# A queue of double score steps across pairs of head pairs, with other filler, score-buffer and rank settings, in attention followed by a low-rank mixer

## The chip, the cores and the metric

The kernel runs on one NeuronCore of a Trainium2 chip; the other cores are unused. The metric is the device time of one execution in microseconds (us), as a median of several. The profile's span, from the first to the last instruction, is a little shorter than that time: the profiled execution took 614.26 us and its span is 612.5 us.

Engine names are those of the profile: PE is TensorE (matmuls; PEld is its weight load), DVE is VectorE, ACT is ScalarE, POOL is GpSimd, SP is SyncE, which here only issues transfers.

## The reference

Attention with a threshold, for 8 batches, 8 heads, 576 rows and head width 64, and behind it a mixer on the 512 joined columns:

```python
scores = scale * q @ k.T                      # 576 x 576 for each of 64 heads
thresh = max(scores) - tau                    # per row
scores = where(scores >= thresh, scores, -1e9) - max(scores)
attn = exp(scores);  attn /= sum(attn) + 1e-09
x = attn @ v                                  # heads joined: 8 x 576 x 512
h = (x.T @ U @ V).T                           # low rank, 32, over the rows
u = x + h
out = u + relu(u @ w_ch1) @ w_ch2             # 512 -> 2048 -> 512
```

Inputs and output are float32. Row maxima have to be exact enough to decide what passes the threshold, so q times k is done in float32; the rest of the matmuls are bf16, v as two bf16 parts.

## The kernel before

The unit of the attention part is a **head pair** (two heads of one batch): four per batch, 32 in all, `p` from 0 to 31. A head pair has 576 rows: four tiles of 128 rows and one of 64; the two 64-row tiles of a pair of head pairs (`p`, `p + 1`) share a step. So each pair of head pairs has nine **score steps**, and the kernel has 144.

The kernel is not written in the order in which it runs. Python code makes a list of tasks, each with an engine, a modelled cost and what it depends on; a list scheduler then picks, engine by engine, what comes next, and only then are the instructions recorded, in that order. What is recorded is fixed: at run time each engine goes through its own list in order and waits on semaphores.

```python
class Order:
    TO_PE = 0.15
    BEGIN = (1.2, 4.5, 0.7, 1.3, 0.7)         # PE, DVE, ACT, POOL, SP: free from
    HOLD = (84.27, 20.8, 39.99, ...)          # one number for each of 9 phases
    KEPT = ((), (0, 1, 3, 4), (0, 1, 2, 3, 4, 5))   # PSUM banks of a step: none, one, two
    OFF = { "copy_main": (19.13, -43.29, ...), ... }   # a rank for each kind of task and phase
    ...
        def rank(c):
            ...
            return (t.ready + t.off, s)       # the smallest goes first
    ...
            if e == PE:
                n = free[0]
                while at[PE] + 0.45 < s and last[n] <= at[PE]:
                    self.filler(n)            # a matmul whose result nobody reads
                    at[PE] += 0.22 if at[PE] > 5.5 else 0.43
```

The filler is `fill`, one bf16 matmul of 128x512 with the identity, recorded wherever the model expects PE to idle for over 0.45 us. It keeps PE's clock up and computes nothing.

A score step writes two scores tiles (one for each head) to PSUM. A **double** step does two of them in one go, over all six PSUM banks of the two `trio` tiles; a **single** step uses four banks. Each step has 16 matmuls of 64x64 on the array's quadrants:

```python
    def score_tasks(*steps):                  # one or two steps (p, i)
        def scores(_):
            for slot, (p, i) in enumerate(steps):
                for piece in range(2):
                    for j in range(2):
                        for h in range(2):
                            ...
                            nc.tensor.matmul(cols[part, lo:hi], a.tT[hs, 0, rows],
                                             a.tT[hs, 1, lo:hi], start=True, stop=True)   # L584
        S_ = add(PE, 0.96 * len(steps), scores, deps, kind="S", ...)
        for slot, (p, i) in enumerate(steps):
            step_tasks(p, i, slot, S_, len(steps))
```

Behind it come, for each of the step's two tiles, three passes over 128x576:

```python
    NS = 6
    s_ring = ring("s_sb", NS, [P, S], FP32)
    e_ring = ring("e_sb", NS, [P, S])                    # bf16
    ...
            def weigh(_, ...):                           # DVE, L613: PSUM -> s_sb, and the row's extreme
                nc.vector.tensor_scalar(out=s_sb, in0=score_cols(slot, x), ..., accum_out=m[:, x:x + 1])
            t = add(VEC, 0.678, weigh, [S_, got("w", tiles[0] + x - NS)], frees=[...])
        ...
            def exponential(_, ..., e_sb=e_ring[tiles[0] % NS], s_sb=s_ring[tiles[0] % NS]):   # ACT, L636
                nc.scalar.activation(out=e_sb, in_=s_sb, func=ACT.Exp, ...)
            ex = add(SCA, 0.667, exponential, [mins[x], got("w", tiles[0] - NS)])
            def select(_, ...):                          # DVE, L643: threshold, product, row sum
                nc.vector.scalar_tensor_tensor(out=w_sb[:, 0:S], in0=s_sb, scalar=thr_[:, x:x + 1],
                    in1=e_sb, op0=ALU.is_le, op1=ALU.mult, accum_out=pr.den[:, i, x:x + 1])
```

`got("w", n)` is the `select` of tile `n`: a tile may take a score buffer only once the `select` that read it last is done.

The selected tiles are transposed by DMA (early on some by PE), then multiplied with v (`product`, L743 to L751, in `value_tasks`), normalized, pushed through the low-rank part, and fed to the mixer's two big products, `up` (L916; `rest`, L932, is its 64-row remainder) and `down` (L949), in `mixer_tasks`. They have 1,088 matmuls of 128x512 and can fill PE wherever a batch is ready for them; `DUE`, one number for each batch, says from which PE step on.

The order in which the tasks are made:

```python
    LONE = 2
    for p in range(0, NP, 2):
        prepare_tasks(p)                      # load q, k, v; transpose q and k on PE
        prepare_tasks(p + 1)
        nine = [(p, i) for i in range(NT)] + [(p + 1, i) for i in range(4)]
        n = 0
        while n < 9:
            two = p >= LONE and n             # the first of nine stays single
            score_tasks(*nine[n:n + (2 if two else 1)])
            n += 2 if two else 1
        value_tasks(p)
        value_tasks(p + 1)
        if (p + 1) % NPAIR == NPAIR - 1:
            mixer_tasks(p // NPAIR)
```

Nine is odd, so each pair of head pairs has one single step and four double ones (the first pair has nine single ones).

Of the kernel before, what the change touches and what calls it, by code (L numbers as in the profile page):

```python
# [68 lines left out]
P = 128  # L69
# [6 lines left out]
B, H, S, D = 8, 8, 576, 64  # L76
# [5 lines left out]
NT = 5  # L82
# [8 lines left out]
W1_AT = (1, 4, 6, 9, 11, 14, 16, 19)  # L91
W2_AT = (20, 21, 23, 24, 25, 26, 28, 29)

DUE = (7.75, 80, 1258.25, 220, 779.25, 421.75, 107.5, 873)

# [30 lines left out]
class Order:  # L128
# [3 lines left out]
    LAG = (0.0, 0.07, 0.1, 0.06, 0.0)  # L132
    SLOW = (1.0,) * 5
    TO_PE = 0.15
    BEFORE = 0.45
    PATIENCE = (0, 0.2, 0.1, 0.9, 1.35)


    BEGIN = (1.2, 4.5, 0.7, 1.3, 0.7)
    LANES = 8  # L140
    SHARE = (0.6, 0.4)
    LANDING = (3.1, 1.4)
    SWITCH = {"quadrants": 0.17, None: 0.13}
    PARTS = {"S": "quadrants"}

    HOLD = (84.27, 20.8, 39.99, 23.29, 62.35, 18.34, 53.51, 0.13, 43.1)
    KEPT = ((), (0, 1, 3, 4), (0, 1, 2, 3, 4, 5))


    OFF = {  # L150
        "copy_main": (19.13, -43.29, -8.12, 1.42, -28.78, -25.28, -22.95, 51.41, -45.85),
        "copy_rest": (60.73, 4.11, 41.5, -5.4, -29.64, 13.18, -80.58, -82.36, -26.38),
        "copy_tt": (198.41, -75.7, -33.86, 48.32, 43.85, 100.62, 7.39, -22.81, -38.44),
        "copy_u": (-21.98, 23.28, 116.5, 77.07, -33.95, 19.36, 29.03, -92.86, 6.98),
        "copy_u4": (-14.02, 51.4, 17, 17.47, -40.5, -60.28, -41.34, 103.29, 7),
        "copy_w": (-55.25, -15.23, 222.13, -81.81, -37.73, 188.9, 52.5, -41.28, 57.53),
        "down": (-108.85, 30.21, -20.13, 90.15, -87.01, -79.16, -34.24, -44.29, 29.17),
        "exponential": (-31.87, -48.96, 9.03, -42.56, 174.18, 12.19, 450.6, 189.09, 141.41),
        "finish": (28.37, -76.92, -41.93, 101.63, 56.59, 2.69, -121.7, -34.02, -50.98),
        "first": (-17.99, 10.62, -38.53, 2.6, 67.74, -65.5, 2.83, -19.66, -6.62),  # L160
        "high": (66.93, -13.94, 46.69, 712.1, 60.2, 95.3, 89.97, 88.03, 39.14),
        "inverse": (-26.26, 8.92, 39.77, 95.96, 39.08, 91.45, 463.65, 19.36, 0.65),
        "join": (13.52, 6.42, 53.64, 9.45, 3.36, 1.67, -114.73, 2.82, 39.08),
        "load": (-18.74, 67.06, -50.44, 55.17, 58.64, 82.33, 125.87, 149.78, -25.84),
        "low": (-9.73, -27.81, 40.61, -12.77, 5.4, -48.88, -55.07, -5.58, -26.87),
        "low4": (41.75, 36.85, 84.8, 33.79, 11.84, -6.69, 54.93, 183.24, 6.02),
        "low_part": (34.11, -32.17, 4.8, -1.24, -37.88, -65.32, -18.36, -17.94, 32.22),
        "low_rank": (-14.94, 306.57, -9.99, 33.17, -60.48, -12.24, -11.83, -46.7, -6.24),
        "make": (7.68, -10.52, -21.46, 3.08, -3.94, 16.95, -45.27, 13.88, 128.85),
        "narrow": (-0.28, -20.88, -40.1, -70.82, 16.79, -28.72, 19.58, 6.78, 1.71),  # L170
        "narrow_u": (-40.8, 31.47, -51.68, -32.58, -91.27, -26.3, 41.16, 82.58, 150.13),
        "narrow_u4": (14.28, 67.11, -13.63, 38.96, 69.08, -15.88, 47.54, -1.08, 25.04),
        "norm": (-36.47, 20.94, 161.35, 153.52, 17.7, 32.05, 16.49, -33.48, 39.64),
        "product": (-25.78, 3.36, 107.07, 34.07, -42.31, 23.71, 434.46, 110.74, -31.94),
        "relu": (44.83, -56.9, 29.43, 68.16, -76.53, 48.16, -10.98, -65.64, 20.44),
        "rest": (8.59, -53.71, 2.63, -9.48, -11.11, -0.73, -28.87, -55.87, 44.85),
        "scores": (-93.28, 8.57, -18.04, -47.28, 8.63, -52.95, -23.78, 413.25, 12.79),
        "select": (46.36, 293.14, 35.49, 104.01, 268.55, 52.2, 72.98, 458.57, 76.64),
        "send": (-23.34, 51.64, 92.04, 28.49, 36.91, 7.91, -217.4, 116.71, -45.23),
        "spread": (-102.39, 8.5, 9.39, -103.02, -0.46, -2.66, -90.25, 41.8, -45.93),  # L180
        "spread4": (26.63, -29.14, -107.73, -80.42, 55.43, 21.3, 10.43, -96.64, -100.01),
        "spread_v": (-62.05, 41.65, -47.22, -27.41, -38.59, 71.83, -165.61, -55.1, -78.6),
        "sum_u": (-55.36, 122.9, 45.74, 86.89, 15.92, 19.31, 4.11, 28.68, 42.79),
        "sum_u4": (15.44, 21.98, -56.37, 5.74, -50.96, -32.03, -61.24, 1.51, 8.11),
        "sums": (27.18, -39.86, -41.27, 101.93, 22.18, 54.82, -48.56, -32.18, -32.56),
        "threshold": (21.67, 39.75, 57.31, -114.62, 90.56, 114.55, -29.79, 46.4, 15.18),
        "turn4": (-47.62, -15.25, -30.68, 42.71, -53.87, -22.98, 35.92, 44.06, 19.31),
        "turn_main": (34.7, -53.42, 3.16, -104.58, -21.66, 79.99, 120.4, 29.72, 83.93),
        "turn_pe": (64.97, 45.46, -130.42, 85.1, 783.71, 163.63, -9.74, -23.06, 24.73),
        "turn_rest": (-89.01, 57.73, -34.88, -49.83, -30.63, 450.94, -36.86, -120.61, -31.99),  # L190
        "turn_u": (45.94, -3.77, -33.34, -53.57, -41.76, -35.51, 29.3, 1351.91, -155.36),
        "turn_w": (27.84, 6.6, -10.51, -30.89, 13.25, 5.13, -98.42, -39.84, 75.01),
        "twin": (4.39, -28.65, 54.86, 6.83, 27.36, 37.94, -39.09, -43.19, -45.42),
        "up": (49.2, -4.95, -54.97, 27.94, 3.9, 179.31, 88.49, -14.97, -39.78),
        "values": (-4.75, -11.18, -30.87, -20.21, -89.93, -8.58, 33.05, 56.9, 16.01),
        "weigh": (16.47, -218.81, -43.72, 80.8, 58.98, -59.6, -10.99, 13.81, 42.45),
        "weights": (-138.85, 46.32, -104.74, -59.99, 22.37, -4.15, 9.01, -37.1, -40.33),
    }

    def __init__(self, nbanks, filler):  # L200
# [2 lines left out]
    def add(self, *args, **kw):  # L203
        t = Task(*args, **kw)
        t.phase = self.phase
        t.lag = 0.0 if t.dma else self.LAG[t.engine]
        t.off = self.OFF[t.fn.__name__][self.phase]
        self.tasks.append(t)
        return t

    def run(self):
# [25 lines left out]
        while left:  # L237
# [28 lines left out]
            if e == PE:  # L266
                n = free[0]
                while at[PE] + 0.45 < s and last[n] <= at[PE]:
                    self.filler(n)
                    at[PE] += 0.22 if at[PE] > 5.5 else 0.43  # L270
                    last[n] = at[PE]
                    kind = "fill"
                parts = self.PARTS.get(t.kind)
                if parts != self.PARTS.get(kind):
                    s += self.SWITCH[parts]
                kind = t.kind
# [30 lines left out]
            steps += t.steps  # L307
            for a in t.after:
                a.ready = max(a.ready, t.end + (self.SIGNAL[e] + (0.0 if a.engine else self.TO_PE)
                                           if a.engine != e or t.dma else 0.0) -  # L310
                              (a.lead if e == PE or e == VEC and a.steps else 0.0))
                a.left -= 1
                if not a.left:
                    ready[a.engine].append(a)
# [4 lines left out]
def kernel(  # L319
# [61 lines left out]
    def ring(name, n, shape, dtype=BF16):  # L381
        return [wpool.tile(shape, dtype, name=f"{name}{k}") for k in range(n)]
# [1 line left out]
    qkraw_ring = ring("qkraw", 2, [P, 9, 2, D], FP32)  # L384
    qkT_ring = ring("qkT", 2, [P, 2, S], FP32)
    vh_ring = ring("vh", 2, [P, NT, 2, 2, D])
    NS = 6
    s_ring = ring("s_sb", NS, [P, S], FP32)
    e_ring = ring("e_sb", NS, [P, S])
    m_ring = ring("m", 8, [P, 2], FP32)  # L390
    thr_ring = ring("thr", 8, [P, 2], FP32)
    rec_ring = ring("rec", 4, [P, NT, 2], FP32)
# [208 lines left out]
    def step_tasks(p, i, slot, S_, len_):  # L601
# [30 lines left out]
        thr = add(SCA, 0.19, threshold, mins)  # L632

        for x in range(2):
            def exponential(_, x=x, e_sb=e_ring[tiles[0] % NS], s_sb=s_ring[tiles[0] % NS]):
                nc.scalar.activation(out=e_sb, in_=s_sb, func=ACT.Exp, bias=m[:, x:x + 1],  # L636
                                     scale=-1.0)

            ex = add(SCA, 0.667, exponential, [mins[x], got("w", tiles[0] - NS)])

            def select(_, x=x, w_sb=w_ring[n % (NW // 2)][:, x, :], e_sb=e_ring[tiles[0] % NS],
                       s_sb=s_ring[tiles[0] % NS]):
                nc.vector.scalar_tensor_tensor(  # L643
                    out=w_sb[:, 0:S], in0=s_sb, scalar=thr_[:, x:x + 1], in1=e_sb,
                    op0=ALU.is_le, op1=ALU.mult, accum_out=pr.den[:, i, x:x + 1])
# [385 lines left out]
            piece(W2_AT[c], lambda _, c=c: w2(_, c), 0.7, weights2, 2.0)  # L1031

    weight_loads()
    for p in range(0, NP, 2):
        prepare_tasks(p)
        prepare_tasks(p + 1)
        nine = [(p, i) for i in range(NT)] + [(p + 1, i) for i in range(4)]
        n = 0
        while n < 9:
            two = p >= LONE and n  # L1040
            score_tasks(*nine[n:n + (2 if two else 1)])
            n += 2 if two else 1
        value_tasks(p)
        value_tasks(p + 1)
        if (p + 1) % NPAIR == NPAIR - 1:
            mixer_tasks(p // NPAIR)

# [37 lines left out]
```

## Time and profile before

| | |
|---|---|
| time, median of 3 | 615.04 us (613.98 to 615.18) |
| span of the profiled execution | 612.5 us, PE clock full throughout |
| PE busy | 588.1 us (96%), of which fillers (L418) 23.2 us, 82 matmuls |
| DVE busy | 522.0 us (85%) |
| ACT busy | 467.6 us (76%) |
| POOL busy | 364.9 us (60%) |
| score matmuls (L584) | 2,304, first at 10.9 us, last at 543.0 us |
| DVE `select` (L643) and `weigh` (L613) | 288 each, 238.9 and 203.1 us |

PE's row says 96% for a stage in which it does useful work and for one in which it runs fillers, so it is to be read stage by stage, and with the filler's line beside it. Matmul ends in the trace are modelled, and neighbours overlap; the distance from the start of one group of matmuls to the start of the next is the better measure of what a group costs.

### The profile page before, as it was taken

What the parts mean: (1) busy time and instruction counts of PE and PEld (TensorE: products, weight loads), DVE (VectorE), ACT (ScalarE), POOL (GpSimd) and SP (SyncE); (2) the same over time, 40 slices, a digit from 0 to 9 for tenths busy, and PEclk for the clock granted to TensorE, in tenths of its full rate; (3) what the DMA queues carried; (4) which work ended last, traced back from release to release, by engine and by line L of the source; (5) the groups of instructions that cost most, each with busy time, mean ns of one, the idle gap of its engine ahead of it and who ended that gap; (6) DMA issues with size and microseconds to landing.
All of it is one profiled execution on the core that took longest, in us unless ns stands there. A gap on an engine that the chain in (4) does not pass through costs nothing. (4 is left out here: it accounts for less than half of the span.)

```text
span 612.5 us, 17223 instructions
## 1 busy us (share of the span) xinstructions
PE 588.1 (96%) x6267; PEld 354.1 (58%) x6343; DVE 522.0 (85%) x1399; ACT 467.6 (76%) x983; POOL 364.9 (60%) x596
## 2 busy tenths in 40 slices
PE   7989889999999999999999999999999999999996
PEld 3446565666566655565566665556565656456553
DVE  2999997998989999899998997999998999994101
ACT  3858898998699876897789965898698977885540
POOL 7768776777777757576666665576557643323000
PEclk9999999999999999999999999999999999999999
DMA  6799999666799799868998998878887897656203
GB/s 148 119 157 164 171 159 176 128 129 145 162 165 164 135 169 172 173 129 145 178 171 141 159 166 159 164 117 156 185 145 156 140 159 143 125 93 102 46 16 70
DMA packets 209716, 87.35 MB, mean 143 GB/s; under 512 B 187744, under 2 KB 199984, under 8 KB 209632
## 3 DMA queue, kind: packets, MB, share of 16 engines
q1 hardware_dynamic: 194624, 63.15, 62.6%
q0 software_dynamic: 14048, 22.76, 18.8%
q8 instruction: 50, 0.82, 0.6%
q10 hardware_dynamic: 960, 0.34, 0.2%
q14 instruction: 34, 0.28, 0.2%
HBM read 37.90 MB, written 9.44 MB: 77 GB/s over the span
## 5 line engine op out<-in xcount | busy, mean ns | idle before, releaser
L636 ACT ACTIVATE e_sb<-s_sb,m 128x576 bf16<-128x576 f32 x288 | 218.5, 778 | 42.9 <-DVE s_sb L613 42.2
L643 DVE SCALAR_TENSOR_TENSOR w_ring<-s_sb,thr,e_sb 128x576 bf16<-128x576 f32 x288 | 238.9, 858 | 9.2 <-ACT e_sb L636 5.9
L613 DVE TENSOR_SCALAR_CACHE_REDUCE s_sb<-trio 128x576 f32<-128x576 f32 x288 | 203.1, 750 | 22.5 <-PE trio L584 20.2
L584 PE MATMUL trio<-qkT 64*64 64x288 f32 (+2 forms) x2304 | 164.2, 410 | 1.3 <-DVE x L772 0.3
L661 POOL COPY w_ring<-w_ring 128x128 bf16<-128x128 bf16 (+1 forms) x168 | 72.0, 433 | 128.8 <-DVE w_ring L643 101.7
L584 PEld LDWEIGHTS trio<-qkT 64*64 64x64 f32 x2304 | 83.3, 133 | 58.9 <-issue 7.0
L949 PE MATMUL bank<-W2b,R 128*128 128x512 bf16 x400 | 98.8, 379 | 2.1 <-DVE x L830 0.6
L455 POOL DMA_DIRECT2D qkraw<-in_q_dram x125 | 82.3, 662 | 31.0 <-PE bank L515 25.5
L455 POOL DMA_DIRECT2D qkraw<-in_k_dram x125 | 81.2, 654 | 4.7 <-issue 4.1
L949 PEld LDWEIGHTS <-R 128*128 128x128 bf16 x576 | 53.3, 98 | 53.0 <-issue 2.5
L916 PE MATMUL bank<-uT,W1b 128*128 128x512 bf16 x327 | 81.5, 380 | 0.7
L795 POOL TENSOR_TENSOR x<-x,rec 128x256 f32<-128x256 f32 (+1 forms) x84 | 63.1, 752 | 30.0 <-DVE x L788 23.0
L916 PEld LDWEIGHTS <-W1b 128*128 128x128 bf16 x512 | 47.4, 98 | 57.2 <-issue 6.3
L747 PEld LDWEIGHTS <-wT_ring 128*128 128x128 bf16 x896 | 55.5, 98 | 9.3 <-issue 4.9
L550 POOL TENSOR_TENSOR vh<-vraw_ring,vh 64x128 bf16<-64x128 f32 x64 | 55.7, 870 | 5.5 <-ACT vh L543 0.8
L906 ACT ACTIVATE R<-bank 128x512 bf16<-128x512 f32 x90 | 52.3, 601 | 4.6 <-PE bank L916 3.7
L961 DVE TENSOR_TENSOR o<-bank,x 128x512 f32<-128x512 f32 x27 | 18.5, 685 | 34.1 <-remote 20.4
L747 PE MATMUL bank<-vh,wT_ring 128*128 128x128 bf16 x608 | 43.6, 220 | 1.8 <-POOL vh L550 1.2
L629 ACT ACTIVATE thr<-m,tau_t 128x2 f32<-128x2 f32 x144 | 42.5, 297 | 0.9 <-DVE s_sb L613 0.6
L916 PE MATMUL trio<-uT,W1b 128*128 128x512 bf16 x150 | 38.6, 379 | 1.5 <-issue 0.2
L949 PE MATMUL trio<-W2b,R 128*128 128x512 bf16 x136 | 33.4, 379 | 1.1 <-DVE s_sb L613 0.8
L906 ACT ACTIVATE R<-trio 128x512 bf16<-128x512 f32 x54 | 32.3, 600 | 2.2 <-PE trio L916 1.1
(104 smaller groups left out, 749.4 us busy)
## 6 DMA issues: line engine op xcount, KB each, us to landing
out_dram<-o SPq DMA_DIRECT2D x71, 128.0 KB, 2.6
vraw_ring<-in_v_dram SPq DMA_DIRECT2D x32, 160.0 KB, 3.6
qkraw<-in_k_dram POOLq DMA_DIRECT2D x63, 80.0 KB, 4.5
qkraw<-in_q_dram POOLq DMA_DIRECT2D x62, 80.0 KB, 3.9
vraw_ring<-in_v_dram SPq DMA_DIRECT2D x32, 128.0 KB, 4.2
qkraw<-in_q_dram POOLq DMA_DIRECT2D x63, 64.0 KB, 4.0
qkraw<-in_k_dram POOLq DMA_DIRECT2D x62, 64.0 KB, 4.1
W1b<-in_moe_w_ch_dram POOLq DMA_DIRECT2D x8, 256.0 KB, 4.9
```

The lines of the kernel that those rows point to most:

```text
L455: queue.dma_start(pr.qkraw[part, to, j, :], src[:, j, of, :])
L550: nc.gpsimd.tensor_tensor(out=pr.vh[part, tiles_, :, h, :], in0=raw[part, tiles_], in1=pr.vh[part, tiles_, :, 0, :], op=ALU.subtract)
L584: mm = nc.tensor.matmul(cols[part, lo:hi], a.tT[hs, 0, rows], a.tT[hs, 1, lo:hi], start=True, stop=True)
L613: nc.vector.tensor_scalar(out=s_sb, in0=score_cols(slot, x), scalar1=-scale, scalar2=None, op0=ALU.mult, op1=ALU.min, accum_out=m[:, x:x + 1])
L636: nc.scalar.activation(out=e_sb, in_=s_sb, func=ACT.Exp, bias=m[:, x:x + 1], scale=-1.0)
L643: nc.vector.scalar_tensor_tensor(out=w_sb[:, 0:S], in0=s_sb, scalar=thr_[:, x:x + 1], in1=e_sb, op0=ALU.is_le, op1=ALU.mult, accum_out=pr. ...
L661: nc.gpsimd.tensor_copy(out=w_sb[:, xs, S:640], in_=w_sb[:, xs, 512:S])
L747: nc.tensor.matmul(av[:, 2 * a + j, :], w, pr.vh[:, kt, j, :, :], start=kt == 0, stop=False)
L795: nc.gpsimd.tensor_tensor(out=x, in0=x, in1=over_sum(part), op=ALU.mult)
L906: nc.scalar.activation(out=R2[:, fts, lo:hi], in_=bank[t.got[0]].rearrange("p (f c) -> p f c", c=hi - lo), func=ACT.Relu)
L916: nc.tensor.matmul(bank[t.got[0]], W1b[:, dt, ft * P:(ft + 1) * P], bt.uT[:, dt, :], start=(dt == 0), stop=(dt == 3))
L949: nc.tensor.matmul(ch, R2[:, ft, lo:lo + P], W2b[:, ft, :], start=(ft == 0), stop=(ft == 15))
```

## The change

What it does:

1. **A queue over the border.** From the third pair of head pairs on (p = 4), the ninth step isn't made at once but kept in `left`; with the first step of the next pair of head pairs it makes one double step. Two pairs of head pairs have 18 steps, so nine doubles and no single one. The `value_tasks` of the head pair whose last step was kept come after that double.
2. **Score buffers.** `s_sb` has 7 buffers (6 before), `e_sb` has 4 (6 before). A tile of `s_sb` is 2,304 bytes in a partition, one of `e_sb` 1,152, so the memory is about the same.
3. **Filler count.** The scheduler's model takes PE as free from 3.34 us on (1.2 before) and as running slowly until 7.2 us (5.5 before), so it records another number of fillers.
4. **A model constant.** `SELF = 0.07` us between a DVE task and one that depends on it on DVE itself.
5. **New ranks.** All numbers in `OFF`, `HOLD` and `DUE`: they decide the order on every engine.

What is computed stays the same, tile by tile. The diff without the tables of numbers:

```diff
-DUE = (7.75, 80, 1258.25, 220, 779.25, 421.75, 107.5, 873)
+DUE = (12, 33, 1397.5, 262.5, 1118.25, 128.25, -374.25, 908.5)
 ...
     TO_PE = 0.15
+    SELF = 0.07
+    WARM = 7.2
 ...
-    BEGIN = (1.2, 4.5, 0.7, 1.3, 0.7)
+    BEGIN = (3.34, 4.5, 0.7, 1.3, 0.7)
 ...
-    HOLD = (84.27, 20.8, 39.99, 23.29, 62.35, 18.34, 53.51, 0.13, 43.1)
+    HOLD = (10.37, 45.62, 12.54, 31.77, 63.99, 75.48, 92.52, 0.04, 31.04)
 ...                                          (OFF: all 47 rows of 9 numbers are new)
-                    at[PE] += 0.22 if at[PE] > 5.5 else 0.43
+                    at[PE] += 0.22 if at[PE] > self.WARM else 0.43
 ...
-                                           if a.engine != e or t.dma else 0.0) -
+                                           if a.engine != e or t.dma else self.SELF if e == VEC else 0.0) -
 ...
-    NS = 6
+    NS, NE = 7, 4
     s_ring = ring("s_sb", NS, [P, S], FP32)
-    e_ring = ring("e_sb", NS, [P, S])
+    e_ring = ring("e_sb", NE, [P, S])
 ...
-            def exponential(_, x=x, e_sb=e_ring[tiles[0] % NS], s_sb=s_ring[tiles[0] % NS]):
+            def exponential(_, x=x, e_sb=e_ring[tiles[0] % NE], s_sb=s_ring[tiles[0] % NS]):
 ...
-            ex = add(SCA, 0.667, exponential, [mins[x], got("w", tiles[0] - NS)])
+            ex = add(SCA, 0.667, exponential, [mins[x], got("w", tiles[0] - NE)])
 ...
+    left = []
     for p in range(0, NP, 2):
         prepare_tasks(p)
+        nine = [(p, i) for i in range(NT)] + [(p + 1, i) for i in range(4)]
+        if left:
+            score_tasks(*left, nine.pop(0))
+            value_tasks(p - 1)
         prepare_tasks(p + 1)
-        nine = [(p, i) for i in range(NT)] + [(p + 1, i) for i in range(4)]
-        n = 0
-        while n < 9:
-            two = p >= LONE and n
-            score_tasks(*nine[n:n + (2 if two else 1)])
-            n += 2 if two else 1
+        while len(nine) > (1 if p > LONE else 0):
+            two = p >= LONE and len(nine) < 9 or p > LONE
+            score_tasks(*[nine.pop(0) for _ in range(2 if two else 1)])
+        left = nine
         value_tasks(p)
-        value_tasks(p + 1)
+        if not left:
+            value_tasks(p + 1)
```

More of the change, by code (lines that the diff above doesn't have):

```diff
@@ L144 @@
     PARTS = {"S": "quadrants"}
-    HOLD = (84.27, 20.8, 39.99, 23.29, 62.35, 18.34, 53.51, 0.13, 43.1)
+    HOLD = (10.37, 45.62, 12.54, 31.77, 63.99, 75.48, 92.52, 0.04, 31.04)
     KEPT = ((), (0, 1, 3, 4), (0, 1, 2, 3, 4, 5))
     OFF = {
[L151 to L197, printed above, removed]
@@ new lines @@
+        "copy_main": (46.15, -32.06, -41.13, -21.37, -49.95, 4.46, -0.84, 11.61, -46.82),
+        "copy_rest": (-16.05, -80.81, -144.79, 55.93, -2.2, -66.69, -80.94, 24.97, -11.01),
+        "copy_tt": (21.41, 36.81, -13.55, 26.67, -50.28, 126.41, 97.5, 5.54, 54.67),
+        "copy_u": (-80.64, -91.99, -10.27, -329.85, 23.48, 68.48, 3.18, -6.9, 72.31),
+        "copy_u4": (-5.06, 16.99, -44.05, -50.39, 1.59, -1.8, 84.05, 3.54, 19.56),
+        "copy_w": (-12.58, 115.35, 31.04, -99.01, 2.6, 27.06, -1.3, -39.98, 36.34),
@@ new lines @@
+        "down": (-44.22, -17.03, 47.87, -21.81, 114.85, -37.7, -40.75, -16.08, 10.18),
+        "exponential": (2.31, -30.55, 21.23, -51.12, 45.25, 83.86, 207.18, 173.71, 42.85),
+        "finish": (3.18, 77.39, -55.07, -50.38, -2.62, 25.65, -7.15, 111.34, -2.24),
+        "first": (-16.68, -2.03, 9.31, 50.9, -30.54, -1.1, -8.18, 10.9, -34.27),
+        "high": (-7, 33.73, 17.35, -9.87, 23.19, 28.11, 122.78, 5.01, 56.45),
+        "inverse": (-68.29, -37.91, 67.78, 50.13, -65.11, -44.83, -60.42, -63.97, -66.71),
@@ new lines @@
+        "join": (0.83, 24.23, 21.83, -6.8, 31.85, -70.48, -99.05, -215.64, 19.67),
+        "load": (-20.84, -1.74, 149.41, -61.42, 299.7, -21.6, 233.19, 226, 65.9),
+        "low": (-21.4, -12.94, 19.95, 44.15, -24.3, -42.71, -169.65, -37.32, -220.92),
+        "low4": (31.94, 268.21, 293.16, -12.75, -58.52, 9.34, 54.91, 328.08, -55.85),
+        "low_part": (-75.99, 7.59, -48.82, -32.15, 89.78, 32, -359.82, -13.75, 40.26),
+        "low_rank": (54.79, 126.5, -1.01, -46.78, 18.64, 40.28, -37.14, 33.7, -40.1),
@@ new lines @@
+        "make": (57.26, 43.95, 54.39, -118.61, 15.27, -7.91, -41.25, 18.54, -45.81),
+        "narrow": (36.45, 21.08, -2.73, 18.49, 59.41, -9.87, 38.5, -29.06, -59.04),
+        "narrow_u": (34.2, 73.86, -10.46, -46.04, 20.92, 51.72, -16.13, 27.92, -78.31),
+        "narrow_u4": (-89.26, -78.01, -18.54, -49.17, -0.7, 43.76, 59.85, -37.11, 37.19),
+        "norm": (-48.64, -6.32, -19.51, 4.64, -33.26, 11.99, -71.43, -57.1, -49.79),
+        "product": (48.26, -50.83, -24.53, 14.92, 96.1, -35.79, -271.92, 256.45, 6.1),
@@ new lines @@
+        "relu": (-6.05, 33.5, -38.23, -97.42, 32.49, 41.1, 58.08, -42.69, -51.37),
+        "rest": (22.91, -70.99, 71.89, -2.61, 28.93, 10.47, 33.84, 54.97, 13.69),
+        "scores": (-10.42, 29.16, 12.56, -77.84, 114.86, 37.24, -53.04, 50.74, 108.98),
+        "select": (59.09, 241.52, 121.93, 74.09, 98.86, 88.1, 258.37, 188.12, 124.28),
+        "send": (2.59, 22.77, 60.2, 52.54, -30.71, -59.91, 21.06, 47.96, 64.01),
+        "spread": (-22.87, -32.46, -185.05, -9.9, 12.56, 8.88, -36.38, 61.14, 136.75),
@@ new lines @@
+        "spread4": (34.02, 17.25, -46.28, 15.62, 24.36, -3.4, -69.32, 111.8, -17.26),
+        "spread_v": (-20.45, 75.81, -36.97, 65.89, -38.29, 51.31, 1.35, 37.96, -1.72),
+        "sum_u": (243.46, 37.61, -93.59, -45.89, -3.65, -68.82, -106.17, 3.88, -1.45),
+        "sum_u4": (-17.14, -51.35, 41.59, 50.26, -8.94, -35.16, 54.85, 58.36, -42.13),
+        "sums": (-67.95, 3.91, -52.45, -90.41, -14.9, 21.15, 9.48, -31.27, -17.28),
+        "threshold": (-8.26, 50.54, -1.85, -59.89, -13.02, -83.98, -46.62, 0.42, 65.64),
@@ new lines @@
+        "turn4": (23.38, -50.66, 30.11, -41.58, 83.82, 95.01, 22.65, 26.94, -15.25),
+        "turn_main": (26.96, -21.37, 34.44, -19.96, 78.56, -20.9, -6.55, -73.4, 37.44),
+        "turn_pe": (-10.48, -50.92, -0.23, -108.21, 104.67, 6.5, -159.04, -10.75, -26.17),
+        "turn_rest": (-54.55, 30.73, 40.39, -21.62, -84.45, -79.57, 110.42, -197.93, 4.25),
+        "turn_u": (-61.54, -31.63, 37.95, -53.78, 4.87, 59.33, -38.65, 1410.73, 4.57),
+        "turn_w": (13.67, 31.98, -137.85, -27.31, -92.37, -65.72, 11.55, -61.1, -50.15),
@@ L198 @@
+        "twin": (203.99, -38.75, -55.8, -99.03, 33.06, 13.16, -112.25, -117.27, 53.03),
+        "up": (-10.95, 37.52, -45.11, 40.31, 80.56, 28.98, -6.26, -43.56, 106.05),
+        "values": (66.92, 2.29, 9.57, -156.87, 59.24, 31.43, -47.63, 90.26, 92.49),
+        "weigh": (-69.86, 105.17, -50.12, -53.99, 17.86, -43.5, 85.11, -58.21, 105.92),
+        "weights": (174.24, 50.18, -42.64, 38.44, -6.18, 24.81, 55.58, -58.68, 68.3),
     }
@@ L634, in step_tasks, with select @@
         for x in range(2):
-            def exponential(_, x=x, e_sb=e_ring[tiles[0] % NS], s_sb=s_ring[tiles[0] % NS]):
+            def exponential(_, x=x, e_sb=e_ring[tiles[0] % NE], s_sb=s_ring[tiles[0] % NS]):
                 nc.scalar.activation(out=e_sb, in_=s_sb, func=ACT.Exp, bias=m[:, x:x + 1],
                                      scale=-1.0)
-            ex = add(SCA, 0.667, exponential, [mins[x], got("w", tiles[0] - NS)])
-            def select(_, x=x, w_sb=w_ring[n % (NW // 2)][:, x, :], e_sb=e_ring[tiles[0] % NS],
+            ex = add(SCA, 0.667, exponential, [mins[x], got("w", tiles[0] - NE)])
+            def select(_, x=x, w_sb=w_ring[n % (NW // 2)][:, x, :], e_sb=e_ring[tiles[0] % NE],
                        s_sb=s_ring[tiles[0] % NS]):
```

## Prediction

> **What bounds the kernel now.** I read the views in this order: the page's first part (PE 96%, DVE 85% busy), then the table of busy time by stage, then the chain of work that ended last, the waits, and last the timeline of single groups. The chain of work is 13% PE and 0% of anything else before it stops at 526 us: of the end it says that PE goes from matmul to matmul, of the middle nothing. So the stages have to be read one by one. The table of stages has for each stretch its length, then the busy time (and number of instructions) of PE, PEld, DVE, ACT and POOL, then PE's clock and the DMA share:
>
> ```profile
> 0.00:20.00 20.00, 16.52 (x112) 7.78 (x113) 9.23 (x30) 9.86 (x19) 15.62 (x31) 1.00 0.73 144
> 20.00:100.00 80.00, 72.80 (x991) 45.60 (x993) 76.70 (x213) 64.07 (x126) 59.54 (x105) 1.00 1.04 158
> ...
> 200.00:300.00 100.00, 98.99 (x1040) 58.94 (x1053) 95.86 (x253) 78.36 (x168) 66.64 (x100) 1.00 0.86 156
> ...
> 545.00:612.50 67.50, 62.43 (x479) 35.73 (x484) 18.76 (x40) 29.82 (x61) 7.75 (x13) 1.00 0.30 58
> ```
>
> The same table for the filler's line alone (PE, PEld):
>
> ```profile
> 0.00:20.00 20.00, 9.38 (x30) 3.35 (x31) 1.00 0.73 144
> 20.00:100.00 80.00, 12.39 (x48) 4.04 (x46) 1.00 1.04 158
> 100.00:612.50 512.50, 1.41 (x5) 0.45 (x5) 1.00 0.79 140
> ```
>
> There are three regimes. **Up to 20 us** everything waits for the first loads. **From 20 to 100 us DVE is the bound**: it is busy for 76.70 of 80 us, while PE's 72.80 hold 12.39 us of fillers; there is no mixer work yet to give PE. **From 100 us on PE is the bound**: nearly no filler, 98 to 99 us of each 100 busy, and after the last score matmul (543 us) PE alone works through the rest of the mixer. DVE is close behind: 92 to 96 us of each 100.
>
> Two costs in the timeline carry the working below (start, length, engine, line, shape). A double score step lasts from 226.10 to 228.21, 2.11 us; a single one from 208.62 to 209.75, 1.13 us:
>
> ```profile
> 208.62 1.20 PE L584 MATMUL trio<-qkT 64*64 64x288 f32 x16
> 209.75 0.40 PE L747 MATMUL bank<-vh,wT 128*128 128x128 bf16 x4
> ...
> 226.10 2.17 PE L584 MATMUL trio<-qkT 64*64 64x288 f32 x32
> 228.21 1.04 PE L949 MATMUL bank<-W2b,R 128*128 128x512 bf16 x4
> ```
>
> And PE's first work: 16 fillers, then the transposes of the first q and k:
>
> ```profile
> 3.34 5.77 PE L418 MATMUL trio<-identb 128*128 128x512 bf16 x16 [3.34 <-DVE identb L344]
> 8.95 0.60 PE L515 MATMUL bank<-ident,qkraw 128*128 128x128 f32 x4
> ```
>
> The issues of the first loads show the last of the eight q and k loads of head pair 0 landed at 6.66 us. So the transposes wait for fillers from 6.66 to 8.95 us, not for data.
>
> **What the Trainium skill says.** "TensorE: Matmul & The Clock Gate", "What's actually happening" and "Wait — 56ns, not 53.3ns?": PE starts at half clock and needs some 3.4 us of sustained work to be let up to full; a matmul of 512 columns takes 426.7 ns cold and 215.7 ns warm. The trace agrees: the fillers start 427 ns apart until 7.6 us and 216 ns apart from 7.9 us on. "TensorEngine Tiling (Array Packing)", "Key Properties": changing the tiling mode drains the array. Score steps run in 64x64 mode and everything else in 128x128, so each block of score steps pays a change in and out; the trace agrees, since two single blocks take 2 x 1.13 = 2.27 us and one double 2.11. "Perfetto Trace Analysis", "Optimization Strategy": a kernel may have regimes with different bounds. That is so here, and so a gain has to be booked in its regime.
>
> **The change part by part.** I take counts from the order in which the instructions of the two built programs stand on each engine, and durations from the trace of before.
>
> *Fewer single steps.* Single blocks go from 24 to 10, doubles from 60 to 67; the 2,304 score matmuls stay. Each of the seven new doubles replaces two singles: 2 x 1.13 - 2.11 = 0.16 us, seven times: **-1.1 us**. All seven lie where PE is the bound, so it counts in full. Nothing else of the computation changes in number: 1,088 big mixer matmuls, the products with v, 288 `weigh`, 288 `select`, 288 exponentials.
>
> *The first fillers.* 16 become 9. Nine cold ones from 3.34 us on: 9 x 0.427 = 3.84, so the transposes begin at about 7.2 us and not at 8.95, after the landing at 6.66. That is 1.75 us; since the clock is let up only at about 7.7 us, the first few of nine transposes (109 ns each warm, I take 218 cold) lose some 0.25 us of it. The following stage is bound by DVE, whose first `weigh` is at 12.1 us and waits for this very chain, so the shift should go through to the end: **-1.5 us**. The loads of head pair 1 landed by 12.2 us, and their transposes ran at 12.0 and 14.7, so they allow it.
>
> *The other fillers.* Before the first mixer matmul the numbers are 60 and 60, so the new order isn't expected to idle less there. Later there were 6 (1.41 us busy; the four at 304.7 us took 1.47 us to the next group) and are 4, one of them in the last stage: **-0.7 us**.
>
> *The first mixer matmul* comes after 24 score steps, not 25, at equal other work. One DVE step is some 3.5 us at that time and PE idles or fills for about a fifth of it: **-0.4 us**, and uncertain.
>
> *Buffers.* In the trace 48 of 288 `weigh` started with five tiles not yet selected, so all six `s_sb` in use; the new order lets DVE stand up to seven ahead in 35 cases. On the other side 40 exponentials started before the `select` four tiles back had ended; with four `e_sb` they would have to wait, mostly 1 to 2 us. ACT is 76% busy and has room; the new order is made for four. I book **0**.
>
> *New ranks.* They move mixer work behind the scores: after the last score step there are 268 big mixer matmuls, not 232, so 36 x 0.216 = 7.8 us more of a stage where PE is alone and waits for nobody. The price is that DVE must be through sooner. From the first `weigh` (12.1) to the last `select` (551.2) DVE is busy 506.9 of 539.1 us, idle 32.2; with the last score 10 us earlier and the first `weigh` 1.5 us earlier it may idle some 24. The waits say where they are to come from: 20.2 us of DVE's idle time were for score matmuls that stood behind mixer matmuls on PE, and there are now fewer mixer matmuls to stand behind. I put half of the missing 8 us as possible stalls on PE, against what a re-ranked order saves elsewhere (PE's own idle time between 100 and 545 us is 445.0 - 436.3 = 8.7 us): **-0.8 us** in sum, a guess.
>
> The sum: -1.1 - 1.5 - 0.7 - 0.4 - 0.8 = -4.5 us, so 615.0 becomes **610.5 us**.
>
> **The rivals.** (a) *DVE becomes the bound up to the last score.* For it: 96% busy between 20 and 100 us is about what it reaches when it is the bound, and the new order asks for 95 to 96% over 530 us. Against it: 20 of its 32 idle us are waits for PE. If it holds, DVE's last `select` comes at about 548 us and the longer tail stands behind that: 617 to 620 us. (b) *Only the merges and the start count*, the order as a whole is worth nothing: 612.4. (c) *The ranks are the main thing*: if they take away half of the 8.7 us between 100 and 545 us and a third of the 15.5 us that fillers and their waits take between 10 and 100 us, another 9 us go: 602 to 604. Against it: the number of fillers before the mixer is the same. (d) *Four `e_sb` hold ACT, ACT holds `select`*: up to 40 waits of 1 to 2 us, but ACT's waits are shared with its idle time (145 us): 612 to 615.
>
> **Range and chances.** The countable parts give -3.3 and the uncertain ones -1.2, with (a) and (d) to the one side and (c) to the other. I take 605 to 616 for 8 in 10. Faster by over 2% means under 602.7, which needs all of (c); slower by over 2% means over 627, for which nothing speaks but a wait that I have not seen.
>
> **What would show it.** The first transpose at about 7.2 us and the first `weigh` at 10.5: the start. 77 score blocks, the doubles still 2.11 us: the merges. Filler time about 19 us, down from 23.2. The last score matmul at about 532 us: if it is past 537, DVE or ACT holds PE and (a) or (d) is right, and the waits then name DVE before PE's score matmuls, or ACT's exponential before `select`. DVE's wait for score matmuls should fall from 20.2 to about 12 us. I would be wrong most easily in the ranks, where I have no count to hold to.

## The result, and the profile after

The changed kernel takes **611.44 us** (median of four, 610.81 to 612.94) beside 615.11 before: a ratio of 0.9944, 95% interval 0.9918 to 0.997. Measured again on another occasion, nine times beside 33 of the kernel before, it was 0.9945 (0.9922 to 0.9967). The span of the profiled execution is 609.5 us, 3.0 less than before. The lines of the changed file stand two below those of before: L586 are the score matmuls, L615 `weigh`, L645 `select`, L420 the filler, L951 `down`.

The table of busy time by stage, columns as in the prediction (length; PE, PEld, DVE, ACT, POOL; PE's clock; DMA):

```profile
0.00:20.00 20.00, 16.42 (x111) 7.53 (x111) 11.23 (x36) 10.33 (x20) 18.15 (x33) 1.00 0.69 146
20.00:100.00 80.00, 72.39 (x997) 46.08 (x1000) 73.62 (x206) 65.06 (x130) 58.10 (x104) 0.98 1.08 156
...
200.00:300.00 100.00, 99.50 (x1070) 60.06 (x1066) 97.46 (x262) 81.37 (x172) 67.55 (x105) 1.00 0.95 166
```

The first row has 2.0 us more of DVE's work in it than before: the start is earlier. The second has less of DVE than before (73.62, not 76.70) and a clock of 0.98: something went wrong there. From 100 to 500 us DVE is a little fuller than it was (97.46 here, 95.86 before); PE's rows can't be compared, for a reason given below.

The fillers alone (PE, PEld) fell from 23.2 to 20.4 us (about 19 had been expected):

```profile
0.00:20.00 20.00, 8.78 (x29) 2.98 (x29) 1.00 0.69 146
20.00:100.00 80.00, 10.43 (x41) 3.62 (x40) 0.98 1.08 156
100.00:612.50 512.50, 1.19 (x4) 0.39 (x4) 1.00 0.79 140
```

The start and the last score step in the timeline (start, length, engine, line, shape):

```profile
3.34 3.77 PE L420 MATMUL trio<-identb 128*128 128x512 bf16 x9 [3.34 <-DVE identb L346]
6.94 0.60 PE L517 MATMUL bank<-ident,qkraw 128*128 128x128 f32 x4
...
530.22 2.17 PE L586 MATMUL trio<-qkT 64*64 64x288 f32 x32
532.32 1.90 PE L918 MATMUL bank<-uT,W1b 128*128 128x512 bf16 x8
```

The first transposes begin at 6.94 us instead of 8.95, and the scores end at 532.3 instead of 543.4, as predicted (7.2 and 532). And the clock of 0.98 has its place; the table for two stretches in the second regime:

```profile
54.50:57.90 3.40, 1.78 (x40) 1.00 0.85 155
57.90:61.30 3.40, 3.30 (x29) 1.90 (x33) 2.17 (x8) 2.47 (x5) 2.20 (x5) 0.50 0.62 147
```

(The first row is PE's busy time alone.) PE was busy for 1.78 of 3.40 us, with waits that no filler stood in, and for the next 3.40 us its clock was halved, 0.50. The double score step in that stretch took 3.61 us from its start to the start of the next group, not 2.10, and DVE waited 1.17 us for it:

```profile
58.22 3.68 PE L586 MATMUL trio<-qkT 64*64 64x288 f32 x32
61.83 0.33 PE L530 MATMUL bank<-ident,qkraw 128*128 128x128 f32 x1
61.29 0.76 DVE L615 TENSOR_SCALAR_CACHE_REDUCE s_sb<-trio 128x576 f32<-128x576 f32 x1 [1.17 <-PE trio L586]
```

The chain of work that ended last, on the page, is again nearly PE alone, and reaches further back:

```profile
PE 25%; DVE 1%; issue 1%; ACT 0%; DVEq 0%; ACTq 0%
```

**Where the 3.0 us of span lie.** I took the timeline's groups on PE one by one, from start to next start, and subtracted for each the least that such a group takes (2.10 us a double, 1.13 a single, 216 ns a big mixer matmul, and so on). The least work fell by 1.15 us (the merges). What is above it, fillers and waits together, went in the first 100 us from 33.2 to 32.4, from 100 to 560 us from 21.2 to 19.2, and in the tail from 4.8 to 5.4. These parts add up to 3.35 us and not to 3.0, so each is good to some 0.4 us only. A start that is 2.0 us earlier is worth about 0.8 by 100 us in this execution, which has the half clock in that stretch, and the merges and the middle gave the rest. (PE's busy row can't be used for such small sums: before, 75 of the 1,088 big mixer matmuls are missing from the trace and look like idle time, while all are there after.)

### The profile page after: what moved, and what is told of

It is laid out like the page before. It is cut to its first block, busy times and chain, and to the rows that moved or that the text cites. A ratio compares the mean times of both kernels' runs of the same rounds, so it can differ in the third digit from the quotient of the medians.

```text
span 609.5 us, 17252 instructions
## 1 busy us (share of the span) xinstructions
PE 590.7 (97%) x6334; PEld 356.1 (58%) x6334; DVE 520.8 (85%) x1399; ACT 471.9 (77%) x983; POOL 369.4 (61%) x596
## 5 line engine op out<-in xcount | busy, mean ns | idle before, releaser
L645 DVE SCALAR_TENSOR_TENSOR w_ring<-s_sb,thr,e_sb 128x576 bf16<-128x576 f32 x288 | 234.7, 845 | 7.5 <-ACT e_sb L638 2.7
L615 DVE TENSOR_SCALAR_CACHE_REDUCE s_sb<-trio 128x576 f32<-128x576 f32 x288 | 203.3, 750 | 20.2 <-PE trio L586 18.6
L586 PE MATMUL trio<-qkT 64*64 64x288 f32 (+2 forms) x2304 | 163.9, 412 | 0.4 <-DVE x L774 0.2
L663 POOL COPY w_ring<-w_ring 128x128 bf16<-128x128 bf16 (+1 forms) x168 | 79.5, 481 | 130.0 <-DVE w_ring L645 108.4
L586 PEld LDWEIGHTS trio<-qkT 64*64 64x64 f32 x2304 | 85.2, 134 | 56.3 <-issue 8.1
L951 PE MATMUL bank<-W2b,R 128*128 128x512 bf16 x384 | 90.6, 379 | 0.0
L951 PEld LDWEIGHTS <-R 128*128 128x128 bf16 x576 | 53.9, 98 | 54.7 <-DVE s_sb L615 0.9
L797 POOL TENSOR_TENSOR x<-x,rec 128x256 f32<-128x256 f32 (+1 forms) x84 | 59.9, 716 | 39.0 <-DVE x L790 33.7
L918 PE MATMUL bank<-uT,W1b 128*128 128x512 bf16 x312 | 76.1, 379 | 0.4 <-ACT uT L853 0.3
L918 PE MATMUL trio<-uT,W1b 128*128 128x512 bf16 x200 | 49.6, 379 | 0.0
L951 PE MATMUL trio<-W2b,R 128*128 128x512 bf16 x192 | 45.2, 379 | 0.3 <-DVE s_sb L615 0.3
L963 DVE TENSOR_TENSOR o<-bank,x 128x512 f32<-128x512 f32 x24 | 16.5, 686 | 33.8 <-PE bank L951 31.2
```

What stands on the lines that cost most here:

```text
L586: mm = nc.tensor.matmul(cols[part, lo:hi], a.tT[hs, 0, rows], a.tT[hs, 1, lo:hi], start=True, stop=True)
L615: nc.vector.tensor_scalar(out=s_sb, in0=score_cols(slot, x), scalar1=-scale, scalar2=None, op0=ALU.mult, op1=ALU.min, accum_out=m[:, x:x + 1])
L663: nc.gpsimd.tensor_copy(out=w_sb[:, xs, S:640], in_=w_sb[:, xs, 512:S])
L797: nc.gpsimd.tensor_tensor(out=x, in0=x, in1=over_sum(part), op=ALU.mult)
L918: nc.tensor.matmul(bank[t.got[0]], W1b[:, dt, ft * P:(ft + 1) * P], bt.uT[:, dt, :], start=(dt == 0), stop=(dt == 3))
L951: nc.tensor.matmul(ch, R2[:, ft, lo:lo + P], W2b[:, ft, :], start=(ft == 0), stop=(ft == 15))
```

## The experiments

The theory to test: the gain is a sum of a start that carries through and of small savings on PE in its own regime. Its rivals: the start is eaten before 100 us; the half clock at 58 us costs what it seems to cost; a score block's extra time is not its change of mode; and the ranks are the real change. Each run has its ratio to the kernel before, run on the same chip, with the 95% interval. The lines of each run's file are a little shifted; the tiles' names say what is what (`trio<-qkT` are the score matmuls, `s_sb<-trio` is `weigh`).

**The changed kernel again**, as the base of the next three.

> The changed kernel again, beside the three others on the same chip: 611.4, 3.5 to 4 us below the kernel before, with PE's clock at half for 3.4 us at about 58 us and the last score matmul at about 532 us.

0.9945 (0.9922 to 0.9967), 613.19 us, from 609.8 to 614.5. The clock dipped again, at 60 us, and the scores ended at 535.6, not at 532. The profiled execution, with 612.7 us of span, was the slowest of the nine. Its beginning has a part of the reason:

```profile
3.34 4.02 PE L420 MATMUL trio<-identb 128*128 128x512 bf16 x9 [3.34 <-DVE identb L346]
7.15 1.06 PE L517 MATMUL bank<-ident,qkraw 128*128 128x128 f32 x4
8.01 0.42 PE L530 MATMUL bank<-ident,qkraw 128*128 128x128 f32 x1
8.22 1.02 PE L517 MATMUL trio<-ident,qkraw 128*128 128x128 f32 x4
```

The same instructions as in the profile after, at the same time within 0.2 us; but four transposes take 1.06 us instead of 0.60, because here the clock was let up at 9.1 us and there at 6.7. That makes the first `weigh` 1.04 us later (11.15 and 10.11). More was lost ahead of the dip, where PE waited for the transfer that transposes a selected tile, and DVE with it:

```profile
60.28 0.61 PE L753 MATMUL bank<-vh,wT_ring 128*128 128x64 bf16 x8 [3.91 <-DMA wT_ring<-w_ring]
60.32 0.82 DVE L645 SCALAR_TENSOR_TENSOR w_ring<-s_sb,thr,e_sb 128x576 bf16<-128x576 f32 x1 [2.47 <-DMA wT_ring<-w_ring]
```

In the profile after, the wait for the same transfer was 0.32 us. Why it is long in one execution and short in another stays open.

**The start alone, in the kernel before.**

```diff
     def fill(n):
+        filled[0] += 1
+        if 9 < filled[0] <= 16:
+            return
         nc.tensor.matmul(bank[n]...                 # order otherwise that of before
```

> The kernel before, with 9 of its first 16 fillers and every other instruction in the same order. If the start is worth what the prediction says and goes through DVE's regime to the end: first transposes near 7.0 us, first weigh near 10.1, and 613.2, 1.8 below before. Rival: the loads of head pair 1 or the later fillers take it back, then the first weigh is early and the first mixer matmul still comes at about 91 us, and the time is within 0.4 us of before.

0.9944 (0.9925 to 0.9963), 613.00 us: seven fillers less give by this ratio what the whole change gives; the runs below put it lower. In the trace the first transposes are at 6.58 us, the first `weigh` at 9.75, the first mixer matmul at 89.2 (91.0 before), and the last score step ends at 542.2 (543.4). The start carries through, though not all of it. This run's clock also dipped, from 43.5 to 47.0 us.

**The start undone, in the changed kernel.**

```diff
     def fill(n):
+        filled[0] += 1
+        for _ in range(8 if filled[0] == 9 else 1):      # eight in place of the ninth: 16 first fillers
+            fill_one(n)                                  # the matmul that fill was
```

> The changed kernel with 16 first fillers, order otherwise the same: the start undone alone. If the start carries through: 613.3, 1.9 above the changed kernel. If other waits in the first 100 us would have taken it anyway: within 0.5 us of the changed kernel. The dip of PE's clock at 58 us may move, as the activity is the same but 1.9 us later: if it goes away, 1.5 us less than said.

0.9972 (0.9956 to 0.9988), 613.97 us, 0.8 above the changed kernel by the medians, 1.7 us by the two ratios. The undone start costs less than the 1.9 expected. The dip did not go away: the clock was halved for 6.8 us from 59.6 us on, after PE had waited 2.65 us for a transposed tile. The other reading is the more useful one: with 16 fillers on both sides, queue, buffers and ranks are worth 0.28%, 1.7 us.

**Fillers where PE stood idle, in the changed kernel.** Fifteen at five places between 45 and 58 us:

```diff
+EXTRA = {("low_rank", 1): 5, ("spread", 1): 2, ("turn_pe", 7): 2, ("product", 6): 4, ("turn_pe", 9): 2}
 ...
+                for _ in range(EXTRA.get((name, seen[name]), 0)):
+                    if last[n] <= s:
+                        self.filler(n)
```

> The changed kernel with 15 more fillers at five places between 45 and 58 us at which PE sat idle without one. If PE's idle time there is what let the clock fall to half for 3.4 us: the clock stays full, the double score block at 58 us takes 2.1 us and not 3.7, and the time is 610.0 (1.5 below the changed kernel), a little less gain if the fillers come too late for what they stand before. Rival: the time there is DVE's, and PE's slow block is off the path: the block gets shorter, DVE's select and weigh stay where they are, and the time doesn't change (within 0.4).

0.9931 (0.9908 to 0.9953), 611.48 us, the lowest ratio of all. The clock stays full while PE works, and the double score step is short again. From this run's timeline:

```profile
59.17 2.17 PE L593 MATMUL trio<-qkT 64*64 64x288 f32 x32
```

DVE doesn't wait for that step any more, where it had waited 1.17 us. The last score step ends at 532.2 us, 521.4 after the first `weigh`; in the profile after it was 522.3 and in the repeat 524.4. Beside the repeat, on the same chip, the time is 1.7 us lower by the medians (611.48 and 613.19) and 0.9 by the ratios; 1.5 were expected. But the intervals overlap, and the rerun below gives 0.9943, no better than the changed kernel's 0.9944 and 0.9945. The dip is gone and DVE's wait with it; what that is worth in time is not settled.

**The same for the kernel before with nine fillers**: six more ahead of one product with v, where PE waited 1.67 us for a transposed tile (`EXTRA = {("product", 3): 6}`). And **the run above again**, on the same chip.

> The kernel before with 9 first fillers and six more ahead of one product with v at about 43 us, where PE stood idle for 1.7 us and its clock fell to half for 3.4 us in the run with 9 fillers alone. Order otherwise that of before. If that dip cost time: 1 to 1.5 us less than with 9 fillers alone, 0.9925 of before. If DVE is the bound there and PE's slow stretch is hidden: the same as with 9 fillers, 0.9944.

> The changed kernel with its 15 more fillers again, on the chip of the run before this one: both have 9 first fillers and a full clock, so their difference is what queue, buffers and ranks are worth by themselves. If that is the 2 us that merges and late fillers count to: 0.993 of before less what the other gains, 1 to 2 us below the other run. If the start was all: equal within 0.5 us.

0.9966 (0.9947 to 0.9985), 612.96 us, for the first: the dip is gone (clock full throughout), and nothing is gained over 0.9944; if anything it is the other way. For the second 0.9943 (0.9914 to 0.9972), 611.39 us. So the expectation "1 to 1.5 us less" did not come, and "hidden behind DVE" fits: in that dip DVE was busy for 3.30 of 3.50 us. It holds for that dip and not for the one at 58 us of the changed kernel, where DVE was busy for 2.17 of 3.40 us. The difference of the two, 1.6 us by the medians and 1.8 us by the spans (611.8 and 610.0), is a second measure of queue, buffers and ranks, with nine fillers and a full clock on both sides; the two intervals overlap, but it agrees with the 1.7 us above.

**What the executions say that were not profiled.** Each execution's mean clock over its span was measured, too. Of the 33 executions of the kernel before beside the first four runs, the nine with a clock of 0.999 or more took 612.6 to 614.8 us, and the six with 0.994 or less 617.3 to 619.0. So halved clock and longer time go together in that kernel, and a dip is not hidden everywhere; where those dips lay, no trace shows. It also bears on what the start is worth. On the chip of the last two runs, the executions with a clock of 0.999 or more have medians of 614.2 us for the kernel before (8 of 22), 613.2 with nine fillers and six extra ones (7 of 11) and 610.6 for the changed kernel with its 15 extra fillers (9 of 12): 1.0 us for the start and 2.6 for queue, buffers and ranks. These groups were picked afterwards and are small.

**The price of a change of mode.** In all 67 double steps one unread matmul of 128x128 on the whole array, once between the two halves, once ahead of them:

```diff
             for slot, (p, i) in enumerate(steps):
+                if len(steps) == 2 and slot == 1:      # the other run: slot == 0
+                    nc.tensor.matmul(trio[0][:, 800:928], identb, identb, start=True, stop=True)
```

> The changed kernel with one matmul of 128x128 on the whole array (result unread) between the two halves of each of the 67 double score steps: each double becomes two blocks in 64x64 mode. Against the next run, which has the same 67 matmuls in front of the double: if leaving and entering the mode costs what two single blocks against one double showed, 67 x 0.16 = 11 us more than that run on PE; as some 14 of the doubles lie where DVE is the bound, 8 to 11 us. Rival: a block's extra time is not the mode but its wait for PSUM, then the two runs are within 2 us of each other.

> The changed kernel with the same 67 unread matmuls of 128x128 ahead of the double instead of between its halves: no more changes of mode. 67 x 0.06 = 4 us of PE's time: 614 to 616.

1.0205 (1.016 to 1.025), 628.05 us, for the split, and 0.9981 (0.9965 to 0.9997), 614.73 us, for the one ahead: 13.3 us apart for 67 more changes in and out, 11 expected (eight of the doubles, not 14, lie before 100 us). One such step in the timeline, first split, then with the matmul ahead:

```profile
231.19 1.20 PE L588 MATMUL trio<-qkT 64*64 64x288 f32 x16
232.33 0.23 PE L576 MATMUL trio<-identb 128*128 128x128 bf16 x1
232.49 1.20 PE L588 MATMUL trio<-qkT 64*64 64x224 f32 x16
233.62 0.33 PE L530 MATMUL bank<-ident,qkraw 128*128 128x128 f32 x1
```

```profile
231.78 0.22 PE L576 MATMUL trio<-identb 128*128 128x128 bf16 x1
231.93 2.17 PE L588 MATMUL trio<-qkT 64*64 64x288 f32 x32
234.03 0.40 PE L827 MATMUL bank<-tt,Vb 128*128 128x128 bf16 x4
```

2.43 us from 231.19 to 233.62 and 2.25 from 231.78 to 234.03; as medians over 67 steps 2.426 and 2.252. So 0.174 us for one more exit and entry, 11.7 us for 67; the other 1.6 us are not placed (the split run's clock was also halved for 6.8 us). The rival, a wait for PSUM, would have left the two within 2 us. A second rival is the type, since the unread matmul is bf16 and the scores are float32. On the whole array that change costs nothing: in the split run a bf16 matmul of 512 columns takes 216 ns to the next start whether bf16 or float32 follows, and a float32 transpose 109 ns in both cases. Seven merges are therefore worth 7 x 0.174 = 1.2 us of PE's time.

**The ranks.** The queue off with all else kept; and the new ranks in the kernel before.

```diff
-        while len(nine) > (1 if p > LONE else 0):            # in the changed kernel: the loop of before
+        while n < 9:
 ...                                                          # in the kernel before: OFF, HOLD and DUE of after
```

> The changed kernel without the queue: the loop of before (one single and four doubles in each pair of head pairs), all new ranks, buffers and constants kept. If the queue is worth its seven merges alone: +1.1 us. If the ranks are made for this one order of tasks: the scheduler sets 179 fillers instead of 73, at some 0.28 us each 30 us more: 630 to 645.

> The kernel before with the new tables of ranks and nothing else. If ranks are good or bad by themselves: 1 to 3 us less than before. If they are good only for the task list that they were made for: 289 fillers instead of 82, some 55 us more: 650 to 680.

642.24 us, 1.0443 (1.041 to 1.0476), and 677.66 us, 1.1032 (1.0983 to 1.1081). The new ranks fit only what they were made with: without the queue the time is 26.5 us above the kernel before, and in the kernel before, which lacks the new buffers and model constants as well, 61.9 us above it. The fillers of the first run, by stretch, tell where the order falls apart:

```profile
0.00:100.00 100.00, 23.03 (x83) 7.97 (x83) 1.00 0.95 154
100.00:545.00 445.00, 5.03 (x18) 1.57 (x18) 1.00 0.86 150
545.00:640.00 95.00, 19.12 (x78) 7.04 (x78) 0.99 0.30 57
```

The scores end at 567.9 us there, 35 later than with the queue, and in the tail behind them are only 144 big mixer matmuls (counted by their weight loads), beside 268 with the queue. This measures how ranks fit the rest, not the queue's own worth: the queue, the buffers and the ranks can't be valued one by one with these runs. No run has the queue with the old ranks, or other buffers.

## Why the prediction was right, point by point

610.5 us were predicted and 611.44 measured. By the count above, the part from 100 us on came out near what was booked: 1.1 for merges, 0.7 for fillers and 0.8 for ranks, and in the trace 1.15 + 2.0 - 0.6, of which the 2.0 are waits and not fillers. What is missing lies in the first 100 us, where 1.9 were booked (the start and the first mixer matmul) and 0.8 were found, in an execution with the half clock. That the sum came within 1 us is in part luck: the repeat's median is 613.19, and two readings behind the ranks were wrong (below).

- **The bound and the regimes: right.** One reading was too high: "98 to 99 us of each 100" for PE and "92 to 96" for DVE leave out the stretch from 100 to 200 us, which has 95.98 and 89.09.
- **The merges, -1.1: right.** The step was taken from two blocks in one trace; 67 splits measured 0.174 us each, so 1.2 us.
- **The first fillers, -1.5: in the range of what was measured, too simple in one term.** Alone in the kernel before they gave 1.8 to 2.8 us by the medians (612.96 and 613.00 beside 614.8 and 615.8) and 1.0 where the clock was full, undone in the changed kernel 0.8 to 1.7. The term "some 0.25 us" for cold transposes is not a constant. It depends on when the clock is let up, which in the traces was anywhere from 6.0 to 9.2 us. From the first transpose to the first `weigh` it took 3.17 us when the clock was up by 7 us (or when 16 fillers ran first), 3.6 at 8.1, and 4.0 at 9.1 and 9.2: a loss of 0 to 0.9 us. At the 7.7 us that was assumed the term holds (3.39 in the split run, a loss of 0.22).
- **The other fillers, -0.7: right in count, wrong in size.** From 100 us on, counted to the next group, they took 1.8 us before and 1.4 and 0.3 (in the tail) after: no gain to speak of.
- **The first mixer matmul, -0.4: not seen.** It came 2.0 us earlier, which is the start itself. The half clock at 58 us lies before it; in the two runs without a dip it came 78.0 and 78.7 us after the first `weigh`, beside 78.9 before and after.
- **The buffers, 0: right in effect.** After, ACT's exponential waits for `select` twenty times, 9.2 us in all, where it never did before; four buffers do hold it. DVE's waits for the exponential fell nonetheless, 5.9 to 2.7 us, so it costs nothing on the path. That is read from the traces; no run had other buffers.
- **The ranks, -0.8: about right, for a reason that was half wrong.** DVE idles 26.2 us (530.9 - 504.7) between first `weigh` and last `select`, beside 32.2 before; some 24 were asked for. The idle time was to come out of DVE's wait for score matmuls, from 20.2 to 12 us. It did not. In these lines of before and after (total, times, longest) the longest wait is the one for the very first scores, which ends at the first `weigh`, stands behind no mixer matmul and isn't part of the idle time counted here:

```profile
DVE s_sb L613 <- PE trio L584: 20.2, 16, 8.8
DVE w_ring L643 <- ACT e_sb L636: 5.9, 12, 0.9
...
DVE s_sb L615 <- PE trio L586: 18.6, 18, 6.8
DVE w_ring L645 <- ACT e_sb L638: 2.7, 5, 0.9
```

  Without it the wait for scores was 11.4 us before and 11.8 after. So "20 of its 32 idle us are waits for PE", which was held against rival (a), should have been 11 of 32. What DVE saved came from ACT: 3.2 us from the exponential and 3.0 from the copy that `x` (L788) waits for. PE's own idle time of 8.7 us between 100 and 545 us, on which rival (c) was built, was misread, too: 66 of the 75 missing records lie between 100 and 560 us and look like idle time. In the kernel before with nine fillers, which has the same order and all records, it is 4.7 us (445.0 - 440.3).
- **What was not foreseen**: the half clock at 58 us and, in the repeat, the long wait for a transposed tile ahead of it. The half clock cost 1.5 us on PE and 1.17 on DVE in the profile after; how much of it reached the end is open.

Of the rivals, (a) did not come (last `select` at 541.0, not 548); (b), the merges and start alone, 612.4, is as close as the prediction; (c) did not come.

## What to carry to other kernels

Fillers ahead of the first real matmul should stop when the data lands: seven too many cost 1.0 to 2.8 us here, about as much as the rest of this change brought (1.6 to 2.6). Where a group of matmuls uses another array mode than its neighbours, count the entries and not the matmuls; here one entry is 0.17 us. And a schedule that was tuned with ranks is to be judged with its own ranks only: here half a change, with ranks made for the whole, cost 4 to 10%, which says nothing of the half. Executions that differ by 5 us may differ in their clock: look at it before a change is called faster.

## What the runs showed of the hardware

PE's clock fell to half after a long pause, and without one. In the repeat of the changed kernel, PE waited 3.91 us and the clock was halved for the next 3.4. In the profile after, the longest single wait between 44 and 58 us is 1.42 us; the clock fell after a stretch of 3.4 us in which PE was busy for 1.78. In the kernel before with nine fillers it fell after one with 1.73 of 3.4, with 1.67 us as its longest wait:

```profile
40.10:43.50 3.40, 1.73 (x27) 1.00 1.14 155
43.50:47.00 3.50, 3.50 (x40) 2.21 (x36) 3.30 (x11) 2.98 (x7) 1.87 (x6) 0.51 1.20 134
```

No share of busy time parts these cases from others. A stretch with 1.84 of 3.4 us (44.2 to 47.6 in the profile after) was followed by a full clock, and so was one with 1.72 (606.4 to 609.8 in the repeat), which is less than 1.73 and 1.78. "TensorE: Matmul & The Clock Gate", "HAM oscillation — how this bites in real kernels", of the Trainium skill speaks of idle gaps over some 3.4 us. The repeat's 3.91 us agree; in the two other cases several shorter waits added up, and there the measurement decides. The same page says in "What's actually happening" that the first release varies from run to run: in these traces it came 2.7 to 5.9 us after the first filler, and in a kernel whose first transposes follow close behind, that alone is up to 0.9 us of spread at the start.
